# Banded attention and a highway layer on one core: memsets moved ahead of the V loads, score matmuls all in 32x64 tiles, relu and gate work shared out anew between ScalarE and VectorE

## The chip, the core and the metric

The program runs on one core of one Trainium2 chip. A core has TensorE (PE in the profile; its weight loads have a row of their own, PEld), VectorE (DVE), ScalarE (ACT), GpSimd (POOL), SyncE (SP), and 16 DMA engines. The metric is the device time of one execution in microseconds. The kernel before takes 169.87 us, the median of 3 runs (167.82 to 170.56). The profiled execution took 168.74 us; its span, from the first instruction to the last, is 167.0 us.

## What is computed

Eight batches with eight heads, 576 positions and 64 columns a head. Attention with a linear distance penalty and a window of 128, and on its result, as 4608 rows of 512, a highway layer.

```python
scores = scale * np.matmul(q, k.transpose(0, 1, 3, 2))
bias = slopes[:, None, None] * (-np.abs(rel))[None]          # rel = query - key
mask = (rel >= 0) & (rel < 128)
attn = softmax(np.where(mask, scores + bias[None], -1e9))
x = (attn @ v).transpose(0, 2, 1, 3).reshape(B * S, H * D)
H = np.maximum(x @ w_h, 0.0)
T = 1.0 / (1.0 + np.exp(-(x @ w_t + b_t)))
out = T * H + (1.0 - T) * x
```

All is in bf16 inside, with sums in f32. The kernel takes T * H + (1 - T) * x as x + T * (H - x), and the sigmoid T as 0.5 * tanh(z / 2) + 0.5.

## The kernel before

Everything is unrolled. The order of the whole program is written out by hand in one string, ORDER: each letter is one step of the next item in that step's list, and a digit after s, p, x, h or z is the first of the PSUM banks that the step writes. Each engine works through its own steps strictly in this order, so a step that has to wait holds up all that comes after it on its engine. Loads are issued on POOL's queue, stores on SP's.

There are 32 score units (batch, half of the heads, half of the keys g) and 36 row blocks of 128 rows (four in a batch, and one more for every two batches, which holds the first 64 rows of both). The letters:

- L, `load`: a q or k tile ("t", 128 partitions x 1152 values, 4 heads), a V piece ("v"; per batch for the first two batches, then for two batches at once), or a weight ("w": w_h, w_t, b_t). f32 in memory, bf16 in the tile. 20 tiles LD take the q and k loads; at most eight loads are in flight.
- S, `setup`: part 0 makes the table of distances REL (POOL iota, then five DVE instructions), parts 1 and 2 the masks MT of the two halves of the heads (ACT, exp of REL times a slope), part 3 the ones column of V's four tiles, the zeroed b_t row, ones0 and the identity (DVE memsets, and an affine_select on POOL).
- T, `tr`: the 32x32 transpose of a q or k tile on DVE (line 156).
- s, `scores` (line 183): the unit's matmuls over 4 banks. Contraction is 32 rows, four heads lie on the four groups of 32 rows, and e takes the two halves of 64. A unit's parts are 128 query columns by 128 keys, which use tiles of 32 rows by 128 columns, and 64-column corners in tiles of 32 by 64; 48 matmuls, each with a weight load of its own.
- e, `soft` (201): exp on ACT out of PSUM. m, `mask` (206): product with MT on DVE. p, `pv` (214, 222, 234): the weights times V, with V's ones column giving the row sum. n, `norm` (247, 248): reciprocal and product on DVE, which write x.
- x, `x_tr` (273): PE transposes of a block's x. c, `x_copy` (278): to SBUF on ACT. h, `mm_h` (283) and z, `mm_z` (296, 298): the two weight products, z with a fifth matmul that adds b_t.
- u, `relu_sub` (288): max(h, 0) - x on DVE out of PSUM. a, `tanh` (302) and t, `to_gate` (306): tanh and 0.5 * tt + 0.5, both on ACT. g, `gate` (310): product on DVE. o, `add_x` (314): plus x on POOL. d, `store` (321, 325): out on SP.

Scores use banks 0 to 3, all other matmuls 4 to 7.

Of the kernel before, what the change touches and what calls it, by code (L numbers as in the profile page):

```python
# [9 lines left out]
P = 128  # L10
NB, NS, NG = 8, 2, 2
NLD, NTR, NPB = 20, 12, 8


ORDER = (
    "LLLLLLSSSSLLLTLTLLs0LTLLLeLs0meTp4Lms0nep6LLnms0LeTp4LnLmx4x5cTp6Lz4nLs0atx6LTh4cez5uLTx"
    "4h7aLgcs0mcz5tuoeTz4Ldgp6aLmas0Lnp4eLh6noh7udx4Ts0cLx5tmh4cgex6uh5uLz7utmcs0LaTz6eLTp4oa"
    "ns0tdmp6ez4ngx5mp6cags0ntox4ez5TLdp6Tcos0anh4eLdTh5Lux6s0cuLz4meLTx5p6ams0cgh4tnoez5TLdp"
    "6utms0ah4egnoz5utLx6dmas0Lcx4gh5Teop6TLdcLs0tnLtz4egLup6oTh5aLdgtnos0z4uLdTx5x6Lch7maz5L"
    "cmeh4uLmp6aus0tnp4eggx6nh7ocp4touds0ndx6egz7gToh4amx5dcz7cTotz5aTLdp6aLgts0noh5euTx6Ldh4"  # L20
    "uz7cuz5matms0aTp6ex4nh5gcp6ms0uoz4neLdgx5mLp6aocs0nz4edmp6Tas0tnh4egx5oux6h7TcLdx4tz5uLc"
    "mtp6cmts0anh4egz5guop6Taodts0np4edmz6nx7map4cs0nx6gh7gToh4cez5uodup6Tdts0anx4x5mch6gz4uc"
    "oeTh5dx6uh7tas0ucz5gemz4op6tadgs0anoh5emdh4p6uttgus0onx5z4cdmtp6agox4nz5cdtgp6aotx4neh5d"
    "gh6oucz7udmz6ap4atx7nh6cgtx4gh5uocz7uodx6ah4gdcox5tz6gduz7oath4cdgaoz5uth4gdaotugdod"
)


def lists():

    units = [(b, s, g) for b in range(NB) for g in range(NG) for s in range(NS)]  # L30
    units[1], units[2] = units[2], units[1]
    blocks = []
    for b in range(NB):
        blocks += [(b, 0), (b, 1)] + ([(b, 4)] if b % 2 else []) + [(b, 2), (b, 3)]
    trs = [(b, s, w) for b in range(NB) for s in range(NS) for w in range(2)]
    loads = []
    for b in range(NB):
        for s in range(NS):
            loads += [("t", b, s, 0), ("t", b, s, 1)]
            if b < 2 or b % 2 == 0:  # L40
                n = 1 if b < 2 else 2
                loads += [("v", b, n, m) for m in ((0, 1, 2), (3, 4))[s]]
        if b == 0:
            loads += [("w", 0), ("w", 1), ("w", 2)]
    by = dict(L=loads, T=trs, S=list(range(4)))
    by.update({k: units for k in "sempn"})
    by.update({k: blocks for k in "xchuzatgod"})
    return by


# [1 line left out]
def kernel(  # L52
# [38 lines left out]
    VA = [cp.tile([P, 2 * H, 5, E], BF16, name=f"va{i}") for i in range(NB // 2)]  # L91
# [3 lines left out]
    bT = cp.tile([P, DM], BF16, name="bT")  # L95
    ident = cp.tile([P, P], BF16, name="ident")
    ones0 = cp.tile([P, P], BF16, name="ones0")
    MT = [cp.tile([P, 4, 448], BF16, name=f"mt{s}") for s in range(NS)]
    REL = cp.tile([P, 448], F32, name="rel")
    PS = pp.tile([P, 8, 512], F32, name="ps")  # L100

    def load(kind, *at):
# [17 lines left out]

    def setup(part):
        if part == 0:
            rel = cp.tile([P, 448], I32, name="rel_i")
            far = cp.tile([P, 448], F32, name="far")
            for o in range(2):
                nc.gpsimd.iota(rel[:, 192 * o : 192 * o + 192], pattern=[[1, 192]], base=64,
                               channel_multiplier=-1)
                nc.gpsimd.iota(rel[0:D, 192 * o + P : 192 * o + 192], pattern=[[1, D]], base=0,
                               channel_multiplier=-1)
            nc.gpsimd.iota(rel[:, 384:448], pattern=[[1, D]], base=0, channel_multiplier=-1)  # L130
# [7 lines left out]
        elif part < 3:  # L138
            s = part - 1
            for a in range(4):  # L140
                nc.scalar.activation(out=MT[s][:, a, :], in_=REL[:], func=ACTF.Exp,
                                     scale=-slopes[4 * s + a])
        else:
            for i in range(NB // 2):
                nc.vector.memset(VA[i][:, :, :, D:E], 1.0)
            nc.vector.memset(bT[:], 0.0)
            nc.vector.memset(ones0[:], 0.0)
            nc.vector.memset(ones0[0:1, :], 1.0)
            nc.vector.memset(ident[:], 1.0)
            nc.gpsimd.affine_select(  # L150
                out=ident[:], in_=ident[:], compare_op=ALU.is_equal, fill=0.0,
                base=0, pattern=[[1, P]], channel_multiplier=-1)

    def tr(b, s, w):
        i = 4 * b + 2 * s + w
# [7 lines left out]
    def scores(b, s, g, bank):  # L163
        QT, KT = (TR[(4 * b + 2 * s + w) % NTR] for w in range(2))
        segs = []
        for o in range(2):
            i = 2 * g + o
            segs.append((P * i, P * i + D, P, 192 * o, 0, P))
        for o in range(2):
            i = 2 * g + o  # L170
            if i == 0:
                segs.append((P, P, P, P, 0, D))
            else:
                segs.append((P * i + P, P * i + P, D, 192 * o + P, 0, D))
                segs.append((P * i - D, P * i + D, D, 192 * o + P, D, D))
        if g == 0:
            segs.append((0, 0, P, 384, 0, D))
        first = True
        for k0, q0, m, col, row, n in segs:
            for e in range(2):  # L180
                for a in range(4):
                    rows = slice(32 * a, 32 * a + 32)
                    nc.tensor.matmul(  # L183
                        out=PS[row : row + m, bank + a, col : col + n],
                        lhsT=KT[rows, k0 : k0 + m, e], rhs=QT[rows, q0 : q0 + n, e],
                        start=first and e == 0, stop=e == 1, tile_position=(32 * a, row),
                        skip_group_check=True)
                first = False

    npt = [0]  # L190

# [60 lines left out]
    XP, XT, PA, PZ, TT, UU, OT = {}, {}, {}, {}, {}, {}, {}  # L252
# [27 lines left out]
    def mm_h(b, i, bank):  # L280
        pa = PA[b, i] = PS[:, bank, :]
        for c in range(NC):
            nc.tensor.matmul(out=pa, lhsT=XT[b, i][:, c, :], rhs=wH[:, c, :],  # L283
                             start=c == 0, stop=c == NC - 1)

    def relu_sub(b, i):
        uu = UU[b, i] = ft.tile([P, DM], BF16, name="uu")
        nc.vector.scalar_tensor_tensor(  # L288
            out=like(uu[:], i), in0=like(PA.pop((b, i)), i), scalar=0.0,
            in1=xview(b, i), op0=ALU.max, op1=ALU.subtract)  # L290
# [13 lines left out]
    def to_gate(b, i):  # L304
        tt = TT[b, i]
        nc.scalar.activation(out=tt[:], in_=tt[:], func=ACTF.Copy, bias=0.5, scale=0.5)  # L306

    def gate(b, i):
        uu = UU[b, i][:]
        nc.vector.tensor_tensor(out=uu, in0=uu, in1=TT.pop((b, i))[:], op=ALU.mult)  # L310
# [6 lines left out]
    def store(b, i):  # L317
# [9 lines left out]
    do = dict(L=load, T=tr, S=setup, s=scores, e=soft, m=mask, p=pv, n=norm, x=x_tr, c=x_copy,  # L327
              h=mm_h, u=relu_sub, z=mm_z, a=tanh, t=to_gate, g=gate, o=add_x, d=store)
    by = lists()
    at = dict.fromkeys(by, 0)  # L330
    steps = iter("".join(ORDER))
    with tc.manual_schedule():
        for step in steps:
# [3 lines left out]
            if step in "spxhz":  # L337
                bank = int(next(steps))
# [34 lines left out]
```

## Time and profile before

| | |
|---|---|
| median of 3 runs | 169.87 us (167.82 to 170.56) |
| profiled execution | 168.74 us, span 167.0 us |
| granted TensorE clock, mean | 0.997 |
| busy, largest first | DVE 134.6, PE 134.0, ACT 111.2, POOL 92.2 us |
| scores, PE | 1536 matmuls in 32 units |
| loads | 15.21 MB on the software queue, 16 DMA engines 83.9% taken by it |
| stores | 9.44 MB on the hardware queue |
| instructions fetched | 21 packets, 0.34 MB |

A busy PE is not a PE at its peak: a matmul's record lasts some 200 to 390 ns while the next one starts 27 to 215 ns after it. So the work of a PE step is read from the time between its first matmul and the first matmul of the next step. Idle time of an engine is listed with who ended it; "issue" means that nothing in the profile ended it.

### The profile page before, as it was taken

The page shows a single profiled execution, that of the slowest core. Times are in us where ns is not written, and L with a number is a line of the kernel's source. Part 1 is how long each engine was busy: PE and PEld are TensorE (multiplying, and loading weights), DVE is VectorE, ACT ScalarE, POOL GpSimd, SP SyncE. Part 2 cuts the span into 40 slices and gives each one's busy share as a digit, 9 for nine tenths or more (in the row PEclk, how much of TensorE's full clock was granted, in tenths as well). Part 3 has the DMA queues.
Part 4 walks back from the last instruction along what each step waited for, and adds up shares of the span by engine and source line. Part 5 has one row for each costly group of instructions (what it writes and reads, how often), then busy time and mean ns, then how long its engine had stood idle before and what let it go on. Part 6 is the DMA issues. An engine that isn't in the chain of part 4 may idle for free.

```text
span 167.0 us, 6262 instructions
## 1 busy us (share of the span) xinstructions
PE 134.0 (80%) x2772; PEld 82.3 (49%) x2772; DVE 134.6 (81%) x213; ACT 111.2 (67%) x149; POOL 92.2 (55%) x106
## 2 busy tenths in 40 slices
PE   0002682999996988979999999999889999999960
PEld 0002561556654645646656465665556556655520
DVE  0357674869899899979999999999979978986560
ACT  3063642198598678669496977679766698687670
POOL 7609915759742593568965870825505233553752
PEclk9999999999999999999999999999999999999998
DMA  3977999999999999999999999296821113231443
GB/s 48 163 95 88 135 200 182 191 188 162 220 180 207 206 173 156 213 117 198 180 242 179 217 258 152 20 192 143 171 94 67 63 67 98 95 129 63 190 119 134
DMA packets 48235, 25.04 MB, mean 150 GB/s; under 512 B 38480, under 2 KB 39504, under 8 KB 48208
## 3 DMA queue, kind: packets, MB, share of 16 engines
q0 software_dynamic: 42960, 15.21, 83.9%
q1 hardware_dynamic: 5248, 9.44, 16.3%
q8 instruction: 21, 0.34, 0.8%
q14 instruction: 6, 0.05, 0.1%
HBM read 30.41 MB, written 9.44 MB: 239 GB/s over the span
## 4 chain that ended last, share of the span: by engine, by line
PE 49%; DVE 26%; DMA 10%; issue 7%; POOL 6%; POOLq 1%; DVEq 0%
PE ps L283 14%; PE ps L296 13%; PE ps L183 8%; DVE tr L156 7%; DMA ld<-in_q_dram 6%; DVE uu L288 5%; DVE p L206 5%; DVE x L248 5%; PE ps L273 4%; PE ps L234 4%; DMA va<-in_v_dram 4%; PE ps L298 3%; PE ps L214 3%; DVE uu L310 2%; POOL va L111 2%
## 5 line engine op out<-in xcount | busy, mean ns | idle before, releaser
L314 POOL TENSOR_TENSOR ot<-uu,x 128x512 f32<-128x512 bf16 x36 | 46.5, 1296 | 54.2 <-DVE uu L310 33.1
L201 ACT ACTIVATE p<-ps 128x1792 bf16<-128x1792 f32 (+1 forms) x32 | 49.9, 1560 | 19.0 <-PE ps L183 18.8
L183 PE MATMUL ps<-tr,tr 32*64 32x64 bf16 (+2 forms) x1536 | 26.8, 211 | 20.7 <-DVE tr L156 15.2
L156 DVE STREAM_TRANSPOSE tr<-ld 128x576 uint32<-128x576 uint32 x32 | 38.9, 1243 | 2.8 <-DMA ld<-in_q_dram 2.8
L296 PE MATMUL ps<-wT,xt 128*128 128x512 bf16 x144 | 38.0, 386 | 0.8 <-DVE uu L288 0.4
L283 PE MATMUL ps<-wH,xt 128*128 128x512 bf16 x144 | 36.2, 380 | 0.2 <-DVE x L248 0.2
L206 DVE TENSOR_TENSOR p<-p,mt 128x1792 bf16<-128x1792 bf16 (+1 forms) x32 | 32.2, 1013 | 2.3 <-ACT p L201 2.3
L183 PEld LDWEIGHTS <-tr 32*128 32x128 bf16 (+1 forms) x1536 | 19.5, 103 | 28.6 <-DVE tr L156 16.2
L278 ACT COPY xt<-ps 128x512 bf16<-128x512 bf16 x36 | 20.9, 586 | 14.4 <-PE ps L273 11.8
L288 DVE SCALAR_TENSOR_TENSOR uu<-ps,x 128x512 bf16<-128x512 f32 x36 | 24.2, 682 | 4.4 <-PE ps L283 3.1
L302 ACT ACTIVATE tt<-ps 128x512 f16<-128x512 f32 x36 | 21.4, 601 | 8.8 <-PE ps L298 8.6
L111 POOL DMA_DIRECT2D va<-in_v_dram x25 | 25.2, 1018 | 0.5 <-DMA va<-in_v_dram 0.4
L248 DVE TENSOR_TENSOR x<-ps,rd 128x512 bf16<-128x512 f32 (+1 forms) x32 | 24.3, 758 | 1.2
L306 ACT ACTIVATE tt<-tt 128x512 f16<-128x512 f16 x36 | 22.6, 634 | 0.2
L296 PEld LDWEIGHTS <-xt 128*128 128x128 bf16 x144 | 12.9, 99 | 14.9 <-issue 1.8
L310 DVE TENSOR_TENSOR uu<-uu,tt 128x512 bf16<-128x512 bf16 x36 | 16.3, 466 | 3.2 <-ACT tt L306 3.0
L283 PEld LDWEIGHTS <-xt 128*128 128x128 bf16 x144 | 12.7, 98 | 11.6 <-issue 0.3
L273 PE MATMUL ps<-ident,x 128*128 128x128 bf16 x144 | 14.0, 225 | 3.5 <-DVE x L248 3.4
L214 PEld LDWEIGHTS <-p 128*128 128x128 bf16 x256 | 12.0, 101 | 8.2 <-issue 3.2
L214 PE MATMUL ps<-va,p 128*128 128x65 bf16 x256 | 14.1, 200 | 2.2 <-issue 0.9
L234 PE MATMUL ps<-va,p 64*64 64x65 bf16 x448 | 14.9, 202 | 0.0
L273 PEld LDWEIGHTS <-x 128*128 128x128 bf16 x144 | 10.0, 100 | 8.7 <-DVE x L248 3.8
(31 smaller groups left out, 69.8 us busy)
## 6 DMA issues: line engine op xcount, KB each, us to landing
out_dram<-ot SPq DMA_DIRECT2D x32, 256.0 KB, 3.4
ld<-in_q_dram POOLq DMA_DIRECT2D x16, 288.0 KB, 8.5
ld<-in_k_dram POOLq DMA_DIRECT2D x16, 288.0 KB, 8.4
va<-in_v_dram POOLq DMA_DIRECT2D x12, 256.0 KB, 10.2
va<-in_v_dram POOLq DMA_DIRECT2D x11, 128.0 KB, 7.6
out_dram<-ot SPq DMA_DIRECT2D x8, 128.0 KB, 3.1
wH<-in_moe_w_h_dram POOLq DMA_DIRECT2D x1, 512.0 KB, 8.3
wT<-in_moe_w_t_dram POOLq DMA_DIRECT2D x1, 512.0 KB, 10.1
```

Source lines behind the costliest of these rows:

```text
L111: nc.gpsimd.dma_start(out=VA[b // 2][0:rows, h : h + n * H, m, 0:D], in_=v[b : b + n, :, m * P : m * P + rows].rearrange("b h p d -> p (b ...
L156: nc.vector.transpose(out=TR[i % NTR][:].rearrange("p s e -> p (s e)").bitcast(U32).rearrange("p (s t) -> p t s", t=NT), in_=LD[i % NLD][: ...
L183: nc.tensor.matmul(out=PS[row : row + m, bank + a, col : col + n], lhsT=KT[rows, k0 : k0 + m, e], rhs=QT[rows, q0 : q0 + n, e], start=firs ...
L201: nc.scalar.activation(out=PB[i][:, :, 0:w], in_=PS[:, bank : bank + 4, 0:w], func=ACTF.Exp, scale=scale)
L206: nc.vector.tensor_tensor(out=p[:, :, 0:w], in0=p[:, :, 0:w], in1=MT[s][:, :, 0:w], op=ALU.mult)
L214: nc.tensor.matmul(out=PS[:, bank + o, a * E : a * E + E], lhsT=me[:, a, 192 * o : 192 * o + P], rhs=VA[b // 2][:, b % 2 * H + 4 * s + a, ...
L248: nc.vector.tensor_tensor(out=X[b, g][:, s, :, 0:n, :], in0=av[:, :, 0:n, 0:D], in1=rd[:, :, 0:n, :].to_broadcast([P, 2, n, D]), op=ALU.mult)
L273: nc.tensor.transpose(out=XP[b, i][:, c * P : (c + 1) * P], in_=xchunk(b, i, c), identity=ident[:])
L283: nc.tensor.matmul(out=pa, lhsT=XT[b, i][:, c, :], rhs=wH[:, c, :], start=c == 0, stop=c == NC - 1)
L288: nc.vector.scalar_tensor_tensor(out=like(uu[:], i), in0=like(PA.pop((b, i)), i), scalar=0.0, in1=xview(b, i), op0=ALU.max, op1=ALU.subtract)
L296: nc.tensor.matmul(out=pz, lhsT=xt[:, c, :], rhs=wT[:, c, :], start=c == 0, stop=False)
L314: nc.gpsimd.tensor_tensor(out=like(ot[:], i), in0=like(UU.pop((b, i))[:], i), in1=xview(b, i), op=ALU.add)
```

## The change

- Set-up. Part 0 is now the DVE memsets, ahead of all V loads; part 1 makes REL and the identity (affine_select right after the iotas); parts 2 and 3 the masks. REL has 256 columns instead of 448, since the two halves of 192 columns were the same; an ACT instruction writes both from one copy, and a second one the last 64 columns, so there are 16 in place of 8.
- Scores. Every matmul is a 32x64 tile: what was one of 128 output partitions is two of 64, and the two halves are issued in turn. A unit has 80 matmuls (g = 0) or 64 (g = 1).
- Highway. For 19 of the 36 blocks a new step r takes relu out of PSUM on ACT into a bf16 tile rr, and u is a subtraction of two bf16 tiles. For 10 blocks a new step k makes the gate from tanh on DVE (`tensor_scalar`) in place of t on ACT.
- Order. ORDER is new throughout. The first four units come as (0, 0, 0), (0, 1, 0), (0, 0, 1), (0, 1, 1); before, the second and the third were exchanged. Loads of batch 0 come as q, k, V piece 0, q, k, V pieces 1 and 2, weights, V pieces 3 and 4; those of other batches as q, k, V pieces 0 to 2, q, k, V pieces 3 and 4.

```diff
+RELU_ACT = (1, 3, 4, 7, 8, 9, 10, 11, 12, 13, 14, 17, 18, 19, 20, 21, 23, 24, 25)
+GATE_DVE = (0, 3, 7, 9, 13, 14, 19, 21, 25, 31)
 ORDER = (
-    "LLLLLLSSSSLLLTLTLLs0LTLLLeLs0meTp4Lms0nep6LLnms0LeTp4LnLmx4x5cTp6Lz4nLs0atx6LTh4cez5uLTx"
...
+    "SLLSSLLLTLLTLSLs0LLTeLLTLms0eLp4ms0Lenp6mLnLx4Ls0cx5Lp6cez4LTh5anh4LTrLms0uLep6uz4nLmx5x"
...
 )
-    units[1], units[2] = units[2], units[1]
...
         if b == 0:
-            loads += [("w", 0), ("w", 1), ("w", 2)]
+            loads += ts[:2] + vs[:1] + ts[2:] + vs[1:3] + [("w", 0), ("w", 1), ("w", 2)] + vs[3:]
+        else:
+            loads += ts[:2] + vs[:3] + ts[2:] + vs[3:]
...
         if part == 0:
+            for i in range(NB // 2):
+                nc.vector.memset(VA[i][:, :, :, D:E], 1.0)
+            nc.vector.memset(bT[:], 0.0)
+            nc.vector.memset(ones0[:], 0.0)
+            nc.vector.memset(ones0[0:1, :], 1.0)
+            nc.vector.memset(ident[:], 1.0)
+        elif part == 1:
+            rel = cp.tile([P, 256], I32, name="rel_i")
+            far = cp.tile([P, 256], F32, name="far")
+            nc.gpsimd.iota(rel[:, 0:192], pattern=[[1, 192]], base=64, channel_multiplier=-1)
+            nc.gpsimd.iota(rel[0:D, P:192], pattern=[[1, D]], base=0, channel_multiplier=-1)
+            nc.gpsimd.iota(rel[:, 192:256], pattern=[[1, D]], base=0, channel_multiplier=-1)
+            nc.gpsimd.affine_select(
+                out=ident[:], in_=ident[:], compare_op=ALU.is_equal, fill=0.0,
+                base=0, pattern=[[1, P]], channel_multiplier=-1)
             nc.vector.tensor_copy(out=REL[:], in_=rel[:])
...
+                nc.scalar.activation(
+                    out=MT[s][:, a, 0:384].rearrange("p (o n) -> p o n", o=2),
+                    in_=REL[:, 0:192].rearrange("p (o n) -> p o n", o=1).to_broadcast([P, 2, 192]),
+                    func=ACTF.Exp, scale=-slopes[4 * s + a])
+                nc.scalar.activation(out=MT[s][:, a, 384:448], in_=REL[:, 192:256],
+                                     func=ACTF.Exp, scale=-slopes[4 * s + a])
...
-            segs.append((P * i, P * i + D, P, 192 * o, 0, P))
...
+            q0 = P * i + D
+            segs.append((P * i, P * i + D, q0, q0, 192 * o, P))
+            segs.append((P * i + P, P * i - D if i else P * i + P + D, q0 + D, q0 if i else q0 + D,
+                         192 * o + P, D))
+        segs.sort(key=lambda x: -x[5])
         if g == 0:
-            segs.append((0, 0, P, 384, 0, D))
+            segs.append((0, D, 0, 0, 384, D))
...
+        for ka, kb, qa, qb, col, n in segs:
             for e in range(2):
+                for row, k0, q0 in ((0, ka, qa), (D, kb, qb)):
+                    for a in range(4):
+                        rows = slice(32 * a, 32 * a + 32)
+                        nc.tensor.matmul(
+                            out=PS[row : row + D, bank + a, col : col + n],
+                            lhsT=KT[rows, k0 : k0 + D, e], rhs=QT[rows, q0 : q0 + n, e],
+                            start=first and e == 0, stop=e == 1, tile_position=(32 * a, row),
+                            skip_group_check=True)
...
+    def relu(b, i):
+        rr = RR[b, i] = fx.tile([P, DM], BF16, name="rr")
+        nc.scalar.activation(out=rr[:], in_=PA.pop((b, i)), func=ACTF.Relu)
+
     def relu_sub(b, i):
         uu = UU[b, i] = ft.tile([P, DM], BF16, name="uu")
+        if (b, i) in RR:
+            nc.vector.tensor_tensor(out=like(uu[:], i), in0=like(RR.pop((b, i))[:], i),
+                                    in1=xview(b, i), op=ALU.subtract)
+            return
...
+    def to_gate_v(b, i):
+        tt = TT[b, i]
+        nc.vector.tensor_scalar(out=tt[:], in0=tt[:], scalar1=0.5, scalar2=0.5, op0=ALU.mult,
+                                op1=ALU.add)
```

More of the change, by code (lines that the diff above doesn't have):

```diff
@@ L12 @@
 NLD, NTR, NPB = 20, 12, 8
+RELU_ACT = (1, 3, 4, 7, 8, 9, 10, 11, 12, 13, 14, 17, 18, 19, 20, 21, 23, 24, 25)
+GATE_DVE = (0, 3, 7, 9, 13, 14, 19, 21, 25, 31)
 ORDER = (
-    "LLLLLLSSSSLLLTLTLLs0LTLLLeLs0meTp4Lms0nep6LLnms0LeTp4LnLmx4x5cTp6Lz4nLs0atx6LTh4cez5uLTx"
[L17 to L24, printed above, removed]
+    "SLLSSLLLTLLTLSLs0LLTeLLTLms0eLp4ms0Lenp6mLnLx4Ls0cx5Lp6cez4LTh5anh4LTrLms0uLep6uz4nLmx5x"
+    "6cLcTz5akh4aLTtp6tLgs0noz5euLdggms0Lh4eTp6LorTs0eondmdax4s0cmp6euh4nx5mp6crkz5nux4Taz6cg"
+    "h5aTotx4p6tuLds0gLh5neLgLz6uLcmLs0ax7eTp4oh6ncods0rTx7eh4Ldumz5cTtp6as0grnh5eoTx4z6Ldcum"
+    "s0aLz4eTLLp6mrs0anh5ekkx4gp6Tors0cnx5tLdz4cmLeh5Lmp6rgaus0notz5eTLdx4h6LgcLz7Taotp4maLds"
+    "0rnLz7eumLx6p4cus0ganh6oeTz7drmx4ax5s0cTp6cz4engh5Ttop6rus0admx5tz4gcnoeh5TLdp6kaus0nLh4"
+    "eLugh6kuox7rms0cz5duegx4mp6cs0naoh4eTz5LdgrTx6oaz7tmcp4daus0tnh6gx7grp4Toch6eudnoz7tLx4m"
+    "dz5cgLrTh4aLaop6mrs0tkdux4ez5nmp6cs0uauh4egnoh5us0Lkrdmx4Lp6cgx5z4ncotp6audgz5enoTx4z6td"
+    "aTx7ch5agz4gcmrh6Taop4rmdts0tx6Toz7cenh6dup4guas0onth7eudz4mh5kaux4mp6ctgs0noz4eup6dgagt"
+    "s0onx4h5codex4x6uh7dmcz5cguoh4ap6gduoz5nz4mdatkp6agx5onh4ctx5gx6dch7uocz4gduz5oath4dagto"
+    "z5uh4gdaotugdod"
 )
@@ L37, in lists @@
     for b in range(NB):
[L38 to L42, printed above, removed]
+        n = 1 if b < 2 else 2
+        vs = [("v", b, n, m) for m in range(5)] if b < 2 or b % 2 == 0 else []
+        ts = [("t", b, s, w) for s in range(NS) for w in range(2)]
         if b == 0:
-            loads += [("w", 0), ("w", 1), ("w", 2)]
+            loads += ts[:2] + vs[:1] + ts[2:] + vs[1:3] + [("w", 0), ("w", 1), ("w", 2)] + vs[3:]
+        else:
+            loads += ts[:2] + vs[:3] + ts[2:] + vs[3:]
     by = dict(L=loads, T=trs, S=list(range(4)))
     by.update({k: units for k in "sempn"})
-    by.update({k: blocks for k in "xchuzatgod"})
+    by.update({k: blocks for k in "xchuzagod"})
+    by["r"] = [blocks[i] for i in RELU_ACT]
+    by["k"] = [blocks[i] for i in GATE_DVE]
+    by["t"] = [bk for i, bk in enumerate(blocks) if i not in GATE_DVE]
     return by
@@ L98 @@
     MT = [cp.tile([P, 4, 448], BF16, name=f"mt{s}") for s in range(NS)]
-    REL = cp.tile([P, 448], F32, name="rel")
+    REL = cp.tile([P, 256], F32, name="rel")
     PS = pp.tile([P, 8, 512], F32, name="ps")
@@ L122, in setup @@
         if part == 0:
[L123 to L130, printed above, removed]
+            for i in range(NB // 2):
[13 more added lines that the diff above has]
+                base=0, pattern=[[1, P]], channel_multiplier=-1)
             nc.vector.tensor_copy(out=REL[:], in_=rel[:])
@@ L137, in setup @@
             nc.vector.tensor_tensor(out=REL[:], in0=REL[:], in1=far[:], op=ALU.add)
-        elif part < 3:
-            s = part - 1
+        else:
+            s = part - 2
             for a in range(4):
[L141 to L152, printed above, removed]
+                nc.scalar.activation(
[4 more added lines that the diff above has]
+                                     func=ACTF.Exp, scale=-slopes[4 * s + a])
     def tr(b, s, w):
@@ L167, in scores @@
             i = 2 * g + o
-            segs.append((P * i, P * i + D, P, 192 * o, 0, P))
[L169 to L175, printed above, removed]
+            q0 = P * i + D
[3 more added lines that the diff above has]
+        segs.sort(key=lambda x: -x[5])
         if g == 0:
-            segs.append((0, 0, P, 384, 0, D))
+            segs.append((0, D, 0, 0, 384, D))
         first = True
-        for k0, q0, m, col, row, n in segs:
+        for ka, kb, qa, qb, col, n in segs:
             for e in range(2):
[L181 to L188, printed above, removed]
+                for row, k0, q0 in ((0, ka, qa), (D, kb, qb)):
[6 more added lines that the diff above has]
+                            skip_group_check=True)
+                if e == 0:
+                    first = False
     npt = [0]
@@ L284, in mm_h @@
                              start=c == 0, stop=c == NC - 1)
+    RR = {}
+    def relu(b, i):
+        rr = RR[b, i] = fx.tile([P, DM], BF16, name="rr")
+        nc.scalar.activation(out=rr[:], in_=PA.pop((b, i)), func=ACTF.Relu)
     def relu_sub(b, i):
         uu = UU[b, i] = ft.tile([P, DM], BF16, name="uu")
+        if (b, i) in RR:
+            nc.vector.tensor_tensor(out=like(uu[:], i), in0=like(RR.pop((b, i))[:], i),
+                                    in1=xview(b, i), op=ALU.subtract)
+            return
         nc.vector.scalar_tensor_tensor(
@@ L327 @@
     do = dict(L=load, T=tr, S=setup, s=scores, e=soft, m=mask, p=pv, n=norm, x=x_tr, c=x_copy,
-              h=mm_h, u=relu_sub, z=mm_z, a=tanh, t=to_gate, g=gate, o=add_x, d=store)
+              h=mm_h, u=relu_sub, z=mm_z, a=tanh, t=to_gate, k=to_gate_v, r=relu, g=gate, o=add_x, d=store)
     by = lists()
```

## The prediction

> **What bounds the kernel now.** I read the totals, then the working time of the engines by stage, the chain of waits, the timeline at the start and around two score units, and the DMA queues.
>
> ```profile
> span 167.0 us, 6262 instructions
> PE 134.0 (80%) x2772; PEld 82.3 (49%) x2772; DVE 134.6 (81%) x213; ACT 111.2 (67%) x149; POOL 92.2 (55%) x106
> ```
> ```profile
> 0.00:15.00 15.00, 0.17 (x8) 0.17 (x12) 5.99 (x16) 5.12 (x9) 8.06 (x19) 1.00 0.82 90
> 15.00:33.00 18.00, 11.68 (x292) 8.60 (x285) 11.98 (x17) 6.82 (x5) 11.54 (x17) 1.00 1.44 176
> ...
> 53.00:73.00 20.00, 16.59 (x412) 10.51 (x405) 18.26 (x27) 14.21 (x17) 10.76 (x10) 1.00 1.35 184
> 73.00:93.00 20.00, 19.37 (x437) 12.16 (x435) 19.26 (x32) 15.89 (x21) 14.76 (x18) 1.00 1.38 186
> ```
> Columns of a stage: its length, then PE, PEld, DVE, ACT, POOL. PE does nothing for 15 us, 11.7 of the next 18, and from 33 us on it is nearly full: 122.2 of the 129.0 us up to the last matmul (which ends near 162.4). DVE is almost as full from 33 to 128 us (89.1 of 95). So there are two prizes: the start, and PE after it.
>
> ```profile
> 6.81 0.17 POOL L130 IOTA rel_i<- 128x64 int32 x1
> 10.66 0.12 DVE L145 MEMSET va<- 128x80 bf16 x1 [1.07 <-DMA va<-in_v_dram]
> 12.41 0.17 DVE L149 MEMSET ident<- 128x128 bf16 x1
> 12.65 0.29 POOL L150 TENSOR_SCALAR_AFFINE_SELECT ident<-ident 128x128 bf16<-128x128 bf16 x1 [5.66 <-DVE ident L149]
> 12.89 0.59 POOL L105 DMA_DIRECT2D ld<-in_k_dram  x1
> ```
> The bracket is the idle time before and who ended it. The memsets of V's ones column wait for the V loads, the ident memset stands behind them, POOL's affine_select waits 5.66 us for that, and every later load queues behind it.
>
> ```profile
> 60.16 0.69 PE L183 MATMUL ps<-tr,tr 32*128 32x128 bf16 x48
> 60.78 1.90 PE L283 MATMUL ps<-wH,xt 128*128 128x512 bf16 x8
> ```
> ```profile
> 66.76 0.85 PE L183 MATMUL ps<-tr,tr 32*128 32x128 bf16 x48 [0.37 <-DVE tr L156]
> 67.54 1.04 PE L283 MATMUL ps<-wH,xt 128*128 128x512 bf16 x4
> ...
> 70.21 0.65 PE L183 MATMUL ps<-tr,tr 32*128 32x128 bf16 x37
> 72.02 0.27 PE L183 MATMUL ps<-tr,tr 32*64 32x64 bf16 x11 [1.16 <-issue]
> ```
> ```profile
> q8 instruction: 21, 0.34, 0.8%
> ```
> A score unit with g = 1 takes PE 0.62 us from its start to the next work, one with g = 0 takes 0.785. The third unit stops for 1.16 us in its middle with nothing to wait for. The single records tell why: of all PE rows (a matmul is two, its weight load and itself), the unexplained stops come at rows 1472, 2240, 4032 and 4288, all 192 more than a multiple of 256, and each ends 2.3 to 2.5 us after one of the 21 packets of 16 KB of the instruction queue started. PE's program arrives 256 rows at a time, one fetch ahead; a stretch that uses up its 256 rows before the next fetch lands stops PE. These four stops cost 4.2 us.
>
> **The change part by part.** Its sum stands against the profiled execution: span 167.0, 168.74 with what lies around it, 1.13 under the median of 169.87.
>
> *Start.* The eight memsets took 1.9 us (10.66 to 12.58); ahead of everything they end near 2.8, and POOL, after two loads and three iotas, reaches affine_select near 3.6 and does not wait. In the DMA records the loads land one behind another: the first q at 5.7, a q or k every 1.4, a V piece every 0.95, the three of w together 6.7 us. In the new order, 5 q or k, 5 V pieces and w lie between the first q and k of batch 1: 5.7 + 7.0 + 4.6 + 6.7 = 24.0, against 28.72. Batch 1's first scores began 4.64 later, at 33.36, behind a cold z step (1.9 us). At best they follow at 24.0 + 1.25 (the transpose), at worst at 28.6; I take 26.6, because norm and transpose (0.9 + 1.25) and two h steps still precede them: -6.8. V pieces 3 and 4 now land behind w (about 21); only the later units need them. By then the new order has done two h and one x more and one pv less (0.87 x 2 + 0.23 - 0.71): -1.4. REL narrows from 448 to 256 columns (2.6 us of DVE to about 1.5) and the masks become 16 ACT instructions (3.84 us before; between 3.84 and 7.7 now, I take 5): both end near 10.5, before the second unit's k has landed (11.0), so they cost nothing; if that k came earlier, the first softs would be late.
>
> *Scores.* In the records four 32x128 tiles on different rows start within 10 ns, and the next four 57 ns later for 128 columns. Where 32x64 tiles in both column halves stand next to each other, eight start every 32 ns for 64 columns. Each change between 128- and 64-wide tiles adds some 90 ns: a g = 1 unit has one inside, a g = 0 unit two, and each has one at its end. All in 32x64 and with the halves in turn: g = 0 has 4 rounds of 57, 6 of 32 and one change: 0.51; g = 1 0.45. The 28 units left save 14 x 0.27 + 14 x 0.17 = 6.2 us of PE. If the halves did not overlap at 128 columns, 4 x 57 ns more per unit would turn this into about a tie (0); I take the overlap seen at 64.
>
> *Program length.* A unit has 48 matmuls before, 80 or 64 after; PE's rows grow from 5,544 to 7,080, so 21 fetches become about 27 and each covers less work. Going through the new order with the steps' spacings (pv 0.70 to 0.96, x 0.23, h 0.87, z 1.08, scores as above), the 256-row stretches after batch 1 has begun hold 4.5, 3.3, 1.2, 6.7, 3.2, 4.7, 2.9, 2.9, 4.8, 4.7, 2.7, 3.2 us of work, and then 3.9, 4.1, 3.9, 4.8, 7.2, 2.6, 3.0, 8.7, 3.5, 4.6, 4.0. The price of a fetch: after a stop the next rows were there 6.1, 3.7, 6.4 and 3.7 us later, the 3.7 where the DMA queue was light; stretches of 3.5, 4.2 and 4.9 us of work took 5.17, 5.95 and 6.26 among loads, but 3.8 and 3.9 took 4.1 without. I take 5.0 (the mean of the four) for the first twelve, which run among loads, and 3.7 for the others: 16.8 + 2.0 of stops, less the 4.2 of now. Other idle of some 0.25 a stretch disappears inside the twelve: -3.0. The ends for the floor among loads are 3.7 and 5.8.
>
> *VectorE and ScalarE.* 19 relu_sub read a bf16 tile instead of PSUM: 682 to 466 ns (the bf16 gate, same shape), -4.1 us on DVE, +19 x 0.60 (the tanh row) = 11.4 on ACT. Ten gates on DVE: no such row; between 0.27 (the 128x256 uint32 memset, same bytes) and 0.47 (the bf16 product), nearest the f32 TENSOR_SCALAR of 395 ns, so 0.35: +3.5 there, -6.3 on ACT. DVE ends at about -0.6, ACT at 117 of some 165 us. Both lie under PE's stops: 0. The new wait, relu_sub on ACT's relu, can stand behind one soft (1.67) with transposes queued after it on DVE; today's ACT waits of DVE are 5.3 us in all, and I count no more. Without PE's stops DVE would be the limit: its 115 us after batch 1's first transposes (near 29) and the 4.6 to the end give 150.7, not lower. POOL's adds and the stores stay; loads keep their place between the adds.
>
> Sum: 168.74 - 6.8 - 1.4 - 6.2 + 18.8 - 4.2 - 3.0 = 165.9.
>
> [...] Fetch: the trace has four stops of 0.55 to 1.3 us. [...] Tiles: 48 score matmuls start within 0.50 us, 10 ns apart. [...]
>
> **Rivals.**
> 1. The fetches are light: the floor stays at 3.7 also among loads. Stops 6.4 + 2.0, absorbed idle 1.5: 168.74 - 14.4 + 8.4 - 4.2 - 1.5 = 157.0; with none at all 150. For it: 3.7 appears twice. Against it: 5.17, 5.95, 6.26, all among loads, which the new order also spreads over most of the run.
> 2. Slower: the fetches are heavy, floor 5.8 (mean of those three). Stops 25.6 + 2.0: 168.74 - 14.4 + 27.6 - 4.2 - 3.0 = 174.7. It decides from a floor of 5.7 on. For it: the packets start up to 4.2 us after the rows before are used; against it: the new order's stretches among loads are partly without a load in flight, as the adds hold POOL back.
> 3. The start doesn't shorten, because the units that now come second need k of the other heads and the loads bind: -6.8 falls away: 172.7. Against it is the idle DMA from 11.4 to 12.9 us.
> 4. The tiles start singly, at the 23 ns of pv's 64x64 ones: 1.9 and 1.6 us a unit, some 33 us more: near 199. Against it are the 32 ns for eight.
>
> **How the numbers follow.** Forecast 0.45 (160 to 171 by itself), rival 1 0.25, rival 2 0.20, rival 3 0.07, rival 4 0.03. Predicted is 165.9. Leaving a tenth on either side, the range is 155 to 174. About 2% is what a measurement of this kernel can tell from no change, so faster is under 166.5 and slower over 173.3: rival 1 and a good half of the forecast give faster 0.50; rivals 2 (most of it) and 4 and an edge give slower 0.22; the rest 0.28.
>
> **What would show it.** First score unit near 9 us, batch 1's near 26.6; no POOL wait on ident; score units of 0.51 and 0.45 us with no gap inside; 27 fetches; PE stops "issue" 256 rows apart summing to about 19 us, most before 95 us, while DVE and ACT show more idle time. Score units over 0.6 us, stops under 9 us or over 25, or DVE full through the middle would prove steps wrong.

## The result and the profile after

The changed kernel is slower: 186.83 us median of 4 runs (186.54 to 187.69), against 169.4 us for the kernel before on the same chip. The ratio is 1.107, with a 95% interval of 1.098 to 1.117. That is also above the whole range that was forecast (155 to 174 us). The profiled execution took 186.58 us, span 184.9, mean granted clock 0.928 (0.997 before). A time given here and below is the median of all runs of a kernel; a ratio compares only runs within 1.5% of the fastest of the same kernel.

Totals, clock by slice and instruction queue, from the page of the changed kernel:

```profile
span 184.9 us, 7771 instructions
...
PE 141.3 (76%) x3508; PEld 90.1 (49%) x3540; DVE 138.2 (75%) x223; ACT 117.6 (64%) x166; POOL 90.5 (49%) x104
...
PEclk9999999999589789966998899999987999999996
...
q8 instruction: 27, 0.44, 1.0%
```

DVE (134.6 us before) and PE (134.0) have a few us more of work than before, spread over 18 us more of time: over the whole span no engine is nearly full now. The fetches are the 27 that were forecast. New is the clock row: it shows 5 to 8 tenths in many slices, where the kernel before had nines up to the end of its work. The records behind it have PE at half clock at 45.4 to 52.3, 62.5 to 65.9, 79.6 to 86.4, 100.0 to 103.5 and 137.6 to 141.0 us, 23.9 us in all before the end.

The same stages as before (length, then PE, PEld, DVE, ACT, POOL; behind them the clock, the DMA share and GB/s):

```profile
0.00:15.00 15.00, 3.35 (x188) 3.05 (x188) 8.93 (x19) 9.08 (x19) 11.73 (x23) 1.00 1.13 148
15.00:33.00 18.00, 13.04 (x308) 8.27 (x309) 10.76 (x17) 7.44 (x9) 10.07 (x13) 1.00 1.63 181
33.00:53.00 20.00, 14.56 (x422) 9.72 (x426) 15.14 (x24) 11.37 (x14) 6.83 (x6) 0.83 1.23 133
...
73.00:93.00 20.00, 14.84 (x370) 10.07 (x373) 12.21 (x20) 12.50 (x17) 8.26 (x11) 0.83 1.07 144
```

The start is better: PE works 3.35 us in the first 15 us (0.17 before). From 33 us on, where PE and DVE had been nearly full (19.37 and 19.26 of 20 us from 73 to 93), PE now works 14.84 and DVE 12.21, and PE's clock is 0.83. More than the gain of the start is lost there.

What POOL does at the start, and two stretches of PE's timeline (start, length, engine, line, operation, count; in brackets the idle time ahead and who ended it):

```profile
3.13 0.17 POOL L141 IOTA rel_i<- 128x64 int32 x1
3.26 0.28 POOL L142 TENSOR_SCALAR_AFFINE_SELECT ident<-ident 128x128 bf16<-128x128 bf16 x1
```
```profile
76.79 0.73 PE L189 MATMUL ps<-tr,tr 32*64 32x128 bf16 x64
77.45 0.39 PE L290 MATMUL ps<-wH,xt 128*128 128x512 bf16 x1
81.12 1.06 PE L290 MATMUL ps<-wH,xt 128*128 128x512 bf16 x2 [3.28 <-issue]
```
```profile
108.99 0.87 PE L189 MATMUL ps<-tr,tr 32*64 32x128 bf16 x80
109.80 0.40 PE L280 MATMUL ps<-ident,x 128*128 128x128 bf16 x4
```

The affine_select follows the iotas at once; the 5.66 us of waiting are gone. A score unit of 64 small tiles takes 0.66 us to the next work, one of 80 takes 0.81: no less than the 0.62 and 0.785 of the wide tiles. And behind the first of them, PE stops for 3.28 us between two matmuls of one product, with nothing to wait for. By the weight-load records that is row 3009 of PE's program, which is 193 more than a multiple of 256 (rows are counted from one here, from nought in the prediction).

The waits (total us, times, longest):

```profile
DVE rd L254 <- PE ps L241: 21.4, 14, 5.8
...
PEld L189 <- issue: 16.9, 15, 2.9
...
PE ps L189 <- issue: 11.6, 7, 2.7
...
PEld L290 <- issue: 8.0, 19, 3.2
```

PEld and PE tell of the same stops twice, so these rows are not added up. From single records, the stops at rows 193 above a multiple of 256 are ten. From the weight load before to the one after it is 2.60 us at 15.4 us, then 0.71, 1.34, 2.26, 1.98, 3.28, 2.66, 1.24, 0.54 and 3.02; less the some 0.03 us that two weight loads lie apart anyway, they sum to 19.3 us. Each ends 2.2 to 2.6 us after its instruction packet started. DVE now waits for PE, 21.4 us at the reciprocal alone.

### The profile page after: what moved, and what is told of

It is laid out like the page before. It is cut to its first block, busy times and chain, and to the rows that moved or that the text cites. A ratio compares the mean times of both kernels' runs of the same rounds, so it can differ in the third digit from the quotient of the medians.

```text
span 184.9 us, 7771 instructions
## 1 busy us (share of the span) xinstructions
PE 141.3 (76%) x3508; PEld 90.1 (49%) x3540; DVE 138.2 (75%) x223; ACT 117.6 (64%) x166; POOL 90.5 (49%) x104
## 4 chain that ended last, share of the span: by engine, by line
PE 59%; DVE 17%; issue 13%; DMA 3%; ACT 3%; POOL 2%; POOLq 1%; DVEq 0%
PE ps L290 15%; PE ps L313 13%; PE ps L189 11%; PE ps L241 6%; PE ps L221 5%; DVE p L213 5%; PE ps L280 5%; DVE tr L164 4%; PE ps L315 3%; DMA ld<-in_k_dram 3%; DVE x L255 3%; ACT p L208 2%; DVE uu L305 2%; DVE uu L332 2%; PE ps L229 1%
## 5 line engine op out<-in xcount | busy, mean ns | idle before, releaser
L336 POOL TENSOR_TENSOR ot<-uu,x 128x512 f32<-128x512 bf16 x36 | 45.1, 1261 | 81.6 <-DVE uu L332 55.2
L189 PE MATMUL ps<-tr,tr 32*64 32x64 bf16 (+1 forms) x2304 | 28.7, 226 | 24.2 <-issue 11.6
L290 PE MATMUL ps<-wH,xt 128*128 128x512 bf16 x129 | 39.7, 416 | 4.7 <-issue 4.1
L213 DVE TENSOR_TENSOR p<-p,mt 128x1792 bf16<-128x1792 bf16 (+1 forms) x32 | 37.3, 1168 | 5.6 <-ACT p L208 5.5
L189 PEld LDWEIGHTS <-tr 32*64 32x64 bf16 x2304 | 24.2, 111 | 29.8 <-issue 16.9
L255 DVE TENSOR_TENSOR x<-ps,rd 128x512 bf16<-128x512 f32 (+1 forms) x32 | 24.3, 758 | 1.3
L254 DVE RECIPROCAL rd<-ps 128x8 f32<-128x8 f32 (+1 forms) x32 | 6.6, 207 | 21.6 <-PE ps L241 21.4
L290 PEld LDWEIGHTS <-xt 128*128 128x128 bf16 x144 | 13.6, 104 | 18.7 <-issue 8.0
L313 PEld LDWEIGHTS <-xt 128*128 128x128 bf16 x144 | 13.2, 102 | 14.6 <-issue 3.0
L297 ACT ACTIVATE rr<-ps 128x512 bf16<-128x512 f32 x19 | 11.4, 598 | 13.2 <-PE ps L290 13.2
L305 DVE SCALAR_TENSOR_TENSOR uu<-ps,x 128x512 bf16<-128x512 f32 x17 | 11.6, 683 | 6.4 <-PE ps L290 5.7
L323 ACT ACTIVATE tt<-tt 128x512 f16<-128x512 f16 x26 | 16.1, 629 | 0.3
```

What stands on the lines that cost most here:

```text
L189: nc.tensor.matmul(out=PS[row : row + D, bank + a, col : col + n], lhsT=KT[rows, k0 : k0 + D, e], rhs=QT[rows, q0 : q0 + n, e], start=firs ...
L213: nc.vector.tensor_tensor(out=p[:, :, 0:w], in0=p[:, :, 0:w], in1=MT[s][:, :, 0:w], op=ALU.mult)
L255: nc.vector.tensor_tensor(out=X[b, g][:, s, :, 0:n, :], in0=av[:, :, 0:n, 0:D], in1=rd[:, :, 0:n, :].to_broadcast([P, 2, n, D]), op=ALU.mult)
L313: nc.tensor.matmul(out=pz, lhsT=xt[:, c, :], rhs=wT[:, c, :], start=c == 0, stop=False)
L336: nc.gpsimd.tensor_tensor(out=like(ot[:], i), in0=like(UU.pop((b, i))[:], i), in1=xview(b, i), op=ALU.add)
```

## The experiments

The theory: what costs is the length of PE's program (7,080 rows in place of 5,544), through the fetches and what they bring. The rivals: the small tiles themselves are slow; the work moved to ScalarE or the new order and its loads are to blame; PE just reached a point from which the queue no longer keeps up. Each comparison is with the kernel before, on the same chip. "Stops" are those at rows 193 above a multiple of 256 and over 0.3 us; the kernel before has 4.2 us of long ones, 5.2 in all.

**e1_after_wide.** The changed kernel with the score tiles of before.

```diff
-            q0 = P * i + D
-            segs.append((P * i, P * i + D, q0, q0, 192 * o, P))
...
+            segs.append((P * i, P * i + D, P, 192 * o, 0, P))
...
-                for row, k0, q0 in ((0, ka, qa), (D, kb, qb)):
-                    for a in range(4):
+                for a in range(4):
```

> The changed kernel with the score matmuls as before (48 a unit, 32x128 tiles for the 128-row parts); everything else stays changed. Theory 1 (PE's longer program is the loss: stops at the ends of 256-row fetches, 19.6 us in the changed kernel, and the half clock that follows them): PE's rows fall from 7,080 to 5,544, 21 fetches, the stops fall under 6 us, the granted clock is back above 0.98, score units take 0.79 and 0.62 us, and the time is 157 to 165 us, below both kernels. Theory 2 (the new order, or the work moved to ScalarE, is the loss): it stays over 178 us.

Measured 164.63 us (163.88 to 164.93), ratio 0.977 (0.971 to 0.984). From its page:

```profile
PEclk9999999999569959999999999999999999999996
...
q8 instruction: 21, 0.34, 0.8%
```

Stops sum to 3.4 us, score units take 0.785 and 0.62 us, and batch 1's first unit starts at 25.81 us. Against the forecast of a clock over 0.98, 10.2 us of half clock remain. All of the loss comes with the small tiles, and what is left of the change is a gain of 1.6 to 2.9%.

**e2_before_narrow.** The kernel before with the small tiles alone.

```diff
-            segs.append((P * i, P * i + D, P, 192 * o, 0, P))
...
+            q0 = P * i + D
+            segs.append((P * i, P * i + D, q0, q0, 192 * o, P))
...
+                for row, k0, q0 in ((0, ka, qa), (D, kb, qb)):
```

> The kernel before with only the score matmuls changed to 32x64 tiles (80 or 64 a unit). Theory 1: 27 fetches, stops of 12 us or more in sum against 4.2, score units of about 0.80 and 0.67 us as in the changed kernel, a half clock in places, and 180 to 192 us, as slow as the whole change or slower. Theory 2: within 2% of 169.4 us.

Measured 186.69 us (183.96 to 188.69), ratio 1.098 (1.085 to 1.111), with 21.3 us of stops, 13.6 us of half clock and score units of 0.80 and 0.67 us. The small tiles alone make the loss, also in the old order.

**e3_after_noshare.** The changed kernel with every relu and gate where it was. The order keeps its banks, so some relu_sub read a bank that a later product has overwritten by then; the amount of work is the same.

```diff
-RELU_ACT = (1, 3, 4, 7, 8, 9, 10, 11, 12, 13, 14, 17, 18, 19, 20, 21, 23, 24, 25)
-GATE_DVE = (0, 3, 7, 9, 13, 14, 19, 21, 25, 31)
+RELU_ACT = ()
+GATE_DVE = ()
```

> The changed kernel with no relu on ScalarE and no gate on VectorE (all 36 blocks as before), the rest changed. Theory 1: nothing of weight happens, 183 to 191 us, with the same stops. Theory 2: the work moved between ScalarE and VectorE is the loss, and the time falls under 178 us.

Measured 186.69 us (184.92 to 188.01), ratio 1.104 (1.091 to 1.117), beside 1.107 with the new shares. The new shares of VectorE and ScalarE are worth nothing that can be measured here, in either direction. The stops are not quite the same, though: they sum to 15.0 us in its trace, and waits of PE for DVE and ACT (10.0 us, 6.8 in the changed kernel, without those for the first transposes) take the place of the rest.

**e4_before_setup.** The kernel before with the memsets first and the iotas with the affine_select behind two loads; nothing else.

```diff
-    "LLLLLLSSSSLLLTLTLLs0LTLLLeLs0meTp4Lms0nep6LLnms0LeTp4LnLmx4x5cTp6Lz4nLs0atx6LTh4cez5uLTx"
+    "SLLSLLLLSSLLLTLTLLs0LTLLLeLs0meTp4Lms0nep6LLnms0LeTp4LnLmx4x5cTp6Lz4nLs0atx6LTh4cez5uLTx"
...
+            nc.vector.memset(ident[:], 1.0)
+        elif part == 1:
...
+            nc.gpsimd.affine_select(
```

> The kernel before with only the set-up changed: the VectorE memsets first of all, the iotas and the affine_select behind the first two loads, REL and the masks as before. Expected by the start's part of the prediction: GpSimd's wait of 5.7 us on ident is gone, the third and later loads are issued some 5 us earlier, the first score unit starts between 9 and 12 us in place of 14.8, and the time is 163 to 167 us. Rival: the loads bind the start anyway, and it is within 1% of 169.4 us.

Measured 163.08 us (162.81 to 165.46), ratio 0.968 (0.961 to 0.975): faster than both kernels. PE at the start of batch 1, from its timeline:

```profile
28.24 0.38 PE L298 MATMUL ps<-bT,ones 128*128 128x512 bf16 x1
28.55 0.85 PE L183 MATMUL ps<-tr,tr 32*128 32x128 bf16 x48
```

Batch 1's first unit starts at 28.55 us (33.36 before), 4.8 earlier; the first unit of all at 9.16. There is no half clock. The set-up is the part of the change that gains, and by itself it is at least as good as with the new order and shares (e1).

**e5_before_pad.** The kernel before, wide tiles kept, with 32 (g = 0) or 16 (g = 1) extra matmuls of a single column in each unit, written to a column of the banks that nobody reads. Rows as in the changed kernel: 7,080.

```diff
+                if m == P and n == P:
+                    for x in range(2 if g == 0 else 1):
+                        for a in range(4):
...
+                                out=PS[0:P, bank + a, 448:449],
```

> The kernel before, its tiles kept, with 32 or 16 extra one-column matmuls a score unit (g = 0 or 1) into PSUM columns that nobody reads, so that PE has exactly as many rows as the changed kernel (7,080) but hardly more columns to stream. Theory 1 (the number of rows is the loss: issue and fetch): 27 fetches, stops of 12 us or more, 178 to 190 us, like the kernel before with the narrow tiles alone (186.7). Rival (the 32x64 tiles themselves are slow): under 174 us, score units longer by at most 0.2 us and stops under 8 us.

Measured 189.68 us (187.98 to 190.85), ratio 1.122 (1.113 to 1.131). From its page:

```profile
PEclk9999999999998799699969969999996999999997
...
q8 instruction: 27, 0.44, 1.0%
```

20.5 us of stops, 17 us of half clock. Rows that compute next to nothing cost as much as the small tiles do (ratio 1.122, e2's 1.098): the number of rows is enough to make the loss, and the shape of the tiles is not needed for it. A unit grows too, from 0.785 to 0.99 us and from 0.618 to 0.71: 6.4 and 5.8 ns for each extra pair of a weight load and a one-column matmul.

**e6_after_light and e7_before_light.** The changed kernel, and as a control the kernel before, without the q, k and V loads of batches 2 to 7; these batches use the tiles of the first two.

```diff
+        if kind in "tv" and at[0] > 1:
+            return
...
-                    rhs=VA[b // 2][:, b % 2 * H + 4 * s + a, 2 * g + o, :],
+                    rhs=VA[0][:, b % 2 * H + 4 * s + a, 2 * g + o, :],
```

> The changed kernel without the q, k and V loads of batches 2 to 7: later batches use the tiles of the first two, so the output is left wrong from batch 2 on, and only the DMA traffic of about 30 to 100 us goes. Theory 1 in my form (a fetch among loads takes 5 us and more, without them 3.7): the stops fall from 19.3 to under 9 us, the half clock goes, and the time falls to 163 to 172 us. Rival (the fetch is as slow without loads): over 180 us with stops of 15 us or more.

> The control to that: the kernel before without the q, k and V loads of batches 2 to 7. Theory 1: only its 4 to 5 us of stops and the few waits for loads go, 161 to 167 us. If it falls by as much as the changed kernel does without those loads, the loads cost something other than fetches.

Measured 162.49 us (160.92 to 164.26), ratio 0.960 (0.951 to 0.969), for the changed kernel, and 165.5 us, ratio 0.982 (0.977 to 0.987), for the one before. For the changed kernel that is just under the 163 to 172 us expected. The same loads are worth 24 us to the one and 3.4 us to the other. Stops fall to 4.3 and 1.5 us. The changed kernel without the loads, from its page and then from PE's timeline:

```profile
PEclk9999999999999999999999999999999999999996
...
q8 instruction: 27, 0.44, 1.2%
```
```profile
89.10 0.87 PE L191 MATMUL ps<-tr,tr 32*64 32x128 bf16 x80
89.90 0.29 PE L282 MATMUL ps<-ident,x 128*128 128x128 bf16 x2
```

There are as many fetches as before, but hardly a stop, and the clock is full. 27 fetches leave 4.3 us of stops here, and 19.3 us among all loads. And a score unit still takes 0.80 us, so its length does not come from stops or clock.

**e8_setup_oneswitch.** e4 with the wide tiles of a unit ahead of the narrow ones, one change of width in a g = 0 unit in place of two.

```diff
+        segs.sort(key=lambda x: -x[2])
```

> The kernel before with the set-up memsets first (163.1 us) and the parts of a score unit sorted so that the 32x128 tiles come first and the 32x64 ones last: one change of tile width inside a unit with g = 0 instead of two, same rows. The records give some 90 ns for a change, so units with g = 0 take 0.69 to 0.71 us in place of 0.785, 1.2 to 1.4 us of PE less, and 161.0 to 162.8 us. Rival: VectorE is the limit in the middle, and the time stays within 0.3% of 163.1.

Measured 165.16 us (163.24 to 167.07), ratio 0.969 (0.962 to 0.976): no gain over e4's 0.968. The g = 0 units became shorter, 0.67 us for 0.785. The trace is of the longest run, 167.07 us, and has stops of 9.6 us (5.3 in e4's); the two runs that count for the ratio took 163.24 and 163.50 us. So that stops took up what the units gave is not shown. The time is the one that goes with the rival, VectorE as the limit, which was not tested either.

**e9_wide_light.** e1 without the loads left out in e6.

```diff
+        if kind in "tv" and at[0] > 1:
+            return
```

> The changed kernel with the old score tiles and without the q, k and V loads of batches 2 to 7 (output wrong from batch 2 on). It asks whether the narrow tiles cost anything but fetches. Theory 1 (only the fetches, with the half clock after them): the units are 0.02 to 0.05 us shorter than the narrow ones, and the time is 158 to 162 us, against 162.5 with the narrow tiles. Rival (the narrow tiles have a price of their own): under 157 us.

Measured 158.62 us (157.87 to 159.08), ratio 0.940 (0.932 to 0.949). No stop over 0.3 us. Against e6 it differs in the tiles alone: without the loads, the small tiles still cost 3.9 us (0.960 and 0.940 as ratios, each with its own chip's kernel before). The parts are e6's stops, 4.3, and its longer units, 1.0 (16 x 0.015 + 16 x 0.05), less the 1.3 us that e9's own 3.4 us of half clock cost (the sum below says how that is read): 4.0.

**e10_before_halfpad.** e5 with half of the extra rows, 6,312 in all.

```diff
+                if m == P and n == P and (g == 0 or e == 0):
+                    for a in range(4):
```

> The kernel before with half of the extra one-column matmuls (16 or 8 a unit; 6,312 PE rows, half way between the two kernels). Theory 1: stops of 8 to 15 us and 174 to 184 us, between 169 and 190. Rival (a threshold near the changed kernel's length): within 2% of 169.

Measured 180.9 us (177.21 to 183.0), ratio 1.059 (1.040 to 1.077). Two of the four runs (177.21 and 179.37 us) count for the ratio; the trace, of the run of 182.44 us, has stops of 15.0 us. Half of the extra rows bring about half of e5's loss, so the loss does not set in near the changed kernel's length. A point between 5,544 and 6,312 rows from which it starts is not ruled out.

**e11_after_nov and e12_after_noqk.** The changed kernel without the V loads alone, and without the q and k loads alone, of batches 2 to 7, which use the tiles of the first two batches in their place.

```diff
+        if kind == "v" and at[0] > 1:
+            return
```
```diff
+        if kind == "t" and at[0] > 1:
+            return
```

> The changed kernel without the V loads of batches 2 to 7 (they use batch 0's and 1's; output wrong from there), with all q and k loads. Which loads hold the fetches back? If it is V's many packets of 128 bytes: 163 to 168 us and stops under 8 us. If a fetch waits for whatever is in flight, in proportion to its time on the DMA engines: 168 to 180 us and stops of 8 to 14 us. If it is the q and k packets of 2,304 bytes: over 180 us.

> The other half: the changed kernel without the q and k loads of batches 2 to 7, with all V loads. If V's small packets hold the fetches: over 180 us. If whatever is in flight: 168 to 180 us. If the q and k packets: 163 to 168 us.

Without V the four runs took 181.74, 182.39, 182.50 and 177.13 us. Only the last counts for a comparison, so there is no interval, and the trace is of the first. Without q and k it was 169.28 us (167.13 to 172.25), ratio 0.999 (0.993 to 1.004). In the traces stops are 16.5 and 9.2 us. The load queue's packets, megabytes and share of the 16 DMA engines, without V and then without q and k:

```profile
q0 software_dynamic: 15072, 11.67, 46.2%
```
```profile
q0 software_dynamic: 39504, 8.13, 63.9%
```

V's many small packets hold the DMA engines longer, and yet it is without q and k that the time comes down most. How late the fetches are agrees with that. In the records the rows 193, 449 and so on, 256 apart, are set beside the 27 packets in order: a packet starts over 2.5 us after its row 14 times of 27 in the changed kernel, 10 times without V, 5 without q and k, 3 without either. Both 169.28 and 177.13 us lie in the range expected if a fetch waits for whatever is in flight (168 to 180), but the delay does not go by the time that loads hold the DMA engines. It may go by their bytes: without V 3.54 MB and 9.7 us are gone (186.83 - 177.13), without q and k 7.08 MB and 17.6 us, some 2.5 to 2.7 us for each MB. Whether it is the bytes, the size of the packets or where they fall is not shown.

## Why the prediction was wrong, step by step

*The start (-6.8, -1.4): right, and partly spent.* The memsets end ahead of 3.26 us, the first unit starts at 8.43 (about 9 was forecast), and with fewer rows batch 1's first unit starts at 25.81 (e1; 26.6 forecast). In the changed kernel it starts at 29.36, mostly because a fetch stop of 2.60 us at 15.4 us lies ahead of it. The prediction counted such stops only from batch 1 on: a miss of 2.8 us, most of which is that stop. The -1.4 was not measured by itself; its own terms, 0.87 x 2 + 0.23 - 0.71, give 1.26. Five V pieces at 0.95 us are 4.75 and not 4.6 us. Neither slip matters beside the rest.

*Scores (-6.2): this step failed.* 0.51 and 0.45 us were forecast from how fast tiles start when nothing holds them; 0.80 and 0.67 is what the units take, some 7 us more in all (14 x 0.29 + 14 x 0.22). The prediction's doubt, that the halves might not overlap, was not the reason. The weight loads of the unit at 108.99 us, ns from the unit's start:

```
pairs  1 to  8:    0   3   7  10  13  17  20  23
pairs  9 to 16:   28  33  37  38  42  46  50  52
pairs 17 to 24:   87  91  96  98 100 104 109 111
pairs 25 to 32:  146 148 153 154 159 162 166 168
pairs 33 to 40:  203 274 283 291 299 308 315 323
pairs 41 to 48:  332 340 348 357 365 374 382 391
...
pairs 73 to 80:  599 608 616 624 633 641 649 658
```

The first 32 pairs start as forecast, in rounds of eight every 57 ns or so. From pair 34 on there is one pair every 8.3 ns, a row every 4.2 ns, and the 46 steps from pair 34 to pair 80 take 0.384 us. The pace changes after 33 pairs, 66 rows, that start within 0.20 us; at 4.2 ns each some 48 rows would. In this unit the step from 128 to 64 columns falls on the same pair, but it is not the reason. After the stop that ends at 119.38 us, ten pairs of 128 columns and 22 of 64 start within 0.15 us, and from the 34th on it is 8.3 ns again; after the one that ends at 74.55 us, 32 pairs of 64 columns start within 0.12 us. What sets either pace is not shown. In e5 an extra one-column pair cost 6.4 and 5.8 ns, so a pair has a price there too that does not come from its columns. The prediction had 48 matmuls within 0.50 us, 10 ns apart; it did not ask how long that rate can be kept up.

*Program length (+18.8 - 4.2): near in size.* 27 fetches, and stops of 19.3 us at rows that lie whole blocks of 256 apart. Most of them lie before 95 us, as forecast (12.0 of 19.3). The mechanism is shown by e5 (rows alone: 1.122) and e6 (loads taken away: stops 4.3).

*Other idle absorbed (-3.0): too large.* PE's waits for DVE and ACT, without those for the first transposes, sum to 8.3 us before and 6.8 after: 1.5 us went, not 3.0.

*What was missing: the clock.* The prediction had no term for it, as the kernel before shows none. From PE's timeline of the changed kernel:

```profile
60.09 0.40 PE L280 MATMUL ps<-ident,x 128*128 128x128 bf16 x4
62.44 0.61 PE L221 MATMUL ps<-va,p 128*128 128x65 bf16 x8 [1.95 <-DVE p L213]
```

At 62.5 us, after 1.95 us without work for PE, the clock falls to one half for 3.4 us, and eight matmuls take 0.54 us to the next work, 0.34 elsewhere. The drop at 45.4 us follows two gaps of 1.07 and 0.98 us; those at 79.6, 100.0 and 137.6 come inside or soon after fetch stops of 2.7 us and more. A single gap does not settle it: the stop of 1.98 us that ends at 74.55 us is not followed by a drop. The five drops lie whole multiples of 3.41 us apart, and in the 3.41 us before each of them PE is idle for 1.7 to 2.6 us. Of such steps at full clock, up to the last stretch, the four with 1.95 us of idle time or more were followed by a drop, of the two with 1.73 and 1.82 us only the first, and none with 1.20 us or less; the kernel before has none over 1.23 us and no drop.

*VectorE and ScalarE (0): right in what it costs.* From the groups by line of the changed kernel:

```profile
L297 ACT ACTIVATE rr<-ps 128x512 bf16<-128x512 f32 x19 | 11.4, 598 | 13.2 <-PE ps L290 13.2
...
L302 DVE TENSOR_TENSOR uu<-rr,x 128x512 bf16<-128x512 bf16 x19 | 8.0, 424 | 1.1 <-ACT rr L297 1.1
...
L327 DVE TENSOR_SCALAR tt<-tt 128x512 f16<-128x512 f16 x10 | 3.1, 322 | 0.0
```

598, 424 and 322 ns stand beside the forecast 600, 466 and 350; the relu waits 13.2 us for PE and the subtraction only 1.1 us for the relu. ACT's total came to 117.6 (117 forecast). DVE's rose by 3.6 us instead of falling by 0.6, mainly since the mask products took 1168 ns each (1013 before); they did so in e1 too, but not in e2 (1014), and why is open. e3 shows the whole of it worth nothing.

*The sum.* e6 runs the same rows as the changed kernel, and has no half clock before its last stretch. So the spacings of its weight loads can be set against those of the changed kernel, one by one. Within the 23.9 us of half clock, stops left out, the changed kernel takes 8.7 us more than e6 for the same rows; against the medians of the same steps at full clock in its own trace it is 7.5 us. From e6's profiled execution (162.30) to 186.58 there are 24.3 us, and stops (19.3 - 4.3 = 15.0) with 7.5 to 8.7 of half clock make 22.5 to 23.7 of them. From e1's (164.91), which has the wide tiles, it is units +1.0, stops 19.3 - 3.4 = +15.9, and half clock less the 3.2 us that e1's own costs by its medians, +4.3 to +5.5: 186.1 to 187.3.

Against the prediction's 165.9: scores +7.1, start +2.8, stops behind it 16.7 for 18.8, -2.1, absorption +1.5; that is 175.2. The half clock, for which it had no term, makes it 182.7 to 183.9, and 2.7 to 3.9 us stay without an account. In e2 and e5 the same count (units +1.0 and +4.7, stops less the 5.2 of before, half clock 5.6 and 6.6 by medians) gives 191.4 and 195.3, beside 185.83 and 190.14 in their profiled executions. PE's waits for DVE and ACT, 8.3 us before, are 4.5 and 4.3 there, which is most of the difference.

*The rivals.* Rival 2 (heavy fetches, 174.7) had the sign, but not the reason: it came to a longer time by 27.6 us of stops, where 19.3 were measured, close to the forecast's 18.8. The loss beyond the forecast lies mostly in the scores and the clock, and in these rival 2 does not differ from the forecast. Rival 1 is nearest to what e6 shows with the loads gone. Rival 3 did not occur, and rival 4 neither: tiles do start 3 to 4 ns apart within the first eight pairs of the unit at 108.99 us.

## What to carry to other kernels

Where PE is fed from an unrolled program, count its rows as a resource, beside its columns: more and smaller matmuls brought more fetches here (27 for 21), and among loads PE stopped for 19.3 us at them, without most of the loads for 4.3 (e6). A rate read from a short burst (48 matmuls) must not be carried to a longer one (80) without asking what supplies it. When a forecast adds stops of 2 us to PE, it must allow for the clock too, which was at one half for 23.9 us here; and of a change with several parts, here the one that moved a wait out of the start (e4, 0.968) was worth taking alone.

## What the hardware showed that was not expected

- In the changed kernel, score matmuls of 64 columns start with their weight loads at one pair every 8.3 ns (4.2 ns a row) from the 34th pair on, in the unit at 108.99 us and after the stop that ends at 119.38 us. The first 32 pairs there, and after the stop that ends at 74.55 us, start within 0.12 to 0.17 us.
- PE's clock fell to one half for 3.4 us at 62.5 us, after 1.95 us without work; in e9 it did 1.5 us after a gap of 1.4 us. The changed kernel's five drops lie on steps of 3.41 us: they came after the four steps with 1.95 us of idle time or more and one with 1.73, not after one with 1.82 nor any with 1.20 or less. The 23.9 us of half clock cost the changed kernel 7.5 to 8.7 us.
- Fetches start later among loads (over 2.5 us after their row 14 times of 27, 3 times in e6), but not in proportion to the time that these hold the DMA engines: 169.28 us without the q and k loads, 177.13 (one run) without the V loads, although the load queue took 63.9% of the engines' time with V's and 46.2% with those of q and k.
- From the start of a packet to the end of the stop behind it were 2.2 to 2.6 us among all loads (ten stops of the changed kernel), and 2.3 to 3.5 us in e6 without most of them: this time was not shorter without the loads, the one until the packet starts was.
